# Spreading the last tokens' decays by a TensorE product, and a step's order with its 64-column products together

## The chip, the cores and the metric

The kernel runs on one core of a Trainium2 chip, in one launch. The metric is device time in microseconds (us), the median of three runs. The engines are named as in the profile: PE is TensorE, DVE VectorE, ACT ScalarE, POOL GpSimd and SP the engine that issues most DMAs; PEld is PE's loading of weights.

## What is computed

A gated linear attention over 4 sequences of 768 tokens with 8 heads of 40 columns, then a layer in which each token goes through one of 8 experts, then a gated layer. The change touches only the attention:

```python
for t in range(S):
    kt, vt, qt = (k[:, :, t], v[:, :, t], q[:, :, t])
    m_new = np.maximum(f_gate[:, :, t] + m, i_gate[:, :, t])
    f_stab = np.exp(f_gate[:, :, t] + m - m_new)
    i_stab = np.exp(i_gate[:, :, t] - m_new)
    m = m_new
    C = f_stab[:, :, None, None] * C + i_stab[:, :, None, None] * np.einsum('bhd,bhe->bhde', vt, kt)
    n = f_stab[:, :, None] * n + i_stab[:, :, None] * kt
    h_tilde = np.einsum('bhde,bhe->bhd', C, qt)
    nq = np.einsum('bhd,bhd->bh', n, qt)[:, :, None]
    denom = np.maximum(np.abs(nq), 1.0)
    y[:, :, t] = o * h_tilde / denom
```

## The kernel before

The attention is cut into 24 chunks of 128 tokens, 6 to a sequence. Within a chunk the recurrence becomes products: a matrix of decays between the chunk's tokens, computed on PE from two tables `at` and `rt` (`dec`, L636), goes through exp on ACT (`exp`, L640) and is multiplied on DVE (`pf`, L650) with the products of keys and queries (`sc`, L645). The result meets the values (`out`, L668). What earlier chunks left in the state C is added (`inter`, L677) after it was scaled on DVE (`gs`, L683), and the chunk's own share of the new state is the product `state` (L689). ACT scales the old state by the decay of the chunk's last token (`Cm`, L695, from the tile `gt`), DVE adds the new share (`C`, L703), ACT copies the sum into the layout that `inter` reads (`cb`, L710). Then come the denominators (`abs` L714, `den` L717), the output gate on POOL (`sod`, L722), the result x (L730), its rounding to f16 on ACT (`xh`, L734), the rest in two pieces on POOL and DVE (`xla` L737, `xl` L740), a transposition by five products on PE (`tr`, L746), its copy by ACT (`ev`, L750) and the router's logits (`log`, eight products of L123, and `lg`, L757).

`dec`, `sc`, `out` and their companions work on half of the heads at a time, so they stand twice in a step, as 0 and 1. The products `out`, `inter` and `state` have weights of 64 columns; they go in pairs, one for each half of PE's columns. All other products of a step have weights of 128 columns.

A step n runs all 18 kinds of work once, each for the chunk n minus a lag. The table `ORDER` gives the order and the lags by hand: `out0:1` is `out` for the first half of the heads of the chunk before. Every engine takes its part of a step in this order. `r:k` lets the routing of earlier tokens go on by k small operations, `scat` issues a scatter of finished rows on POOL.

The decays are prepared at the start for two halves of the tokens, x = 0 and 1 (`gates`). `store(x)` writes them to DRAM in two arrays, `L_d` (L516) and `a_d` (L517), from which `decay` loads the tables `at` (L415, L419) and `rt` (L421). `exps(x)` applies exp; its last lines write the decay of each chunk's last token to the DRAM array `G_d` (L529, on ACT's queue) and read it back on SP's queue, broadcast to 64 partitions, twice, into `gt` (L531). `to_end(x)` transposes what is needed by token, with products (L538) and two DVE copies (L540). Chunks 0 and 1 take their decays from SBUF; from chunk 2 on `dec` reads `at` and `rt`, from chunk 3 on their second half (x = 1). In the generator `rest()`, which the `r` entries advance, `store(1)` comes in step 1, and `exps(1)` with the loads of the second half right behind it at that step's end. SP issues in program order, one DMA behind the other.

PSUM tiles of `tr`, `log`, `state`, the routing and `to_end` share two slots (`psC`); `inter` and `out` write into one of two tiles `po`.

Of the kernel before, what the change touches and what calls it, by code (L numbers as in the profile page):

```python
# [9 lines left out]
F32 = mybir.dt.float32  # L10
# [4 lines left out]
ALU = mybir.AluOpType  # L15
# [4 lines left out]
B, H, S, D = 4, 8, 768, 40  # L20
R = B * H
T = 128
NC = S // T
NP = H // 2
# [5 lines left out]
E, F1, F2 = 8, 1024, 1536  # L30
# [7 lines left out]


ORDER = """  # L40
    r:1 tr:3 dec0:0 sc0:0 ev:3 r:2 exp0:0 out0:1 dec1:0 r:1 C:1 sc1:0 pf0:0 sod:2 r:1 x:2 kw:0 r:1 cb:1
    out1:1 exp1:0 r:1 log:3 scat:0 xh:2 r:1 inter:0 pf1:0 abs:1 lg:3 gs:0 state:0 xla:2 r:1 Cm:0 xl:2 den:1
"""
TMAX = (NT - MOST) // T + 1
PITCH = NT + MOST + T
# [14 lines left out]
def fused(ctx, tc, a, out, dbg=None):  # L60
    nc = tc.nc
    V, G, A, PE, SP_ = nc.vector, nc.gpsimd, nc.scalar, nc.tensor, nc.sync
# [3 lines left out]
    perm = ctx.enter_context(tc.tile_pool(name="perm", bufs=1))  # L66
    dram = ctx.enter_context(tc.tile_pool(name="dram", bufs=1, space=DRAM))
# [4 lines left out]
    small = ctx.enter_context(tc.tile_pool(name="small", bufs=2))  # L72
# [4 lines left out]

    c16 = perm.tile([128, 3, 128], F16, name="c16")
    tri, ones, ident16 = (c16[:, i, :] for i in range(3))
    c32 = perm.tile([128, 128 + (NC + 1) * E], F32, name="c32")  # L80
    ident = c32[:, 0:128]
    rev = c32[:, 128:128 + NC * E].rearrange("p (t e) -> p t e", e=E)
    ebase = c32[:, 128 + NC * E:]
    tok = perm.tile([128, NTILE + 1], U32, name="tok")
    ctab = perm.tile([1, E, 2 * TMAX + 4], F32, name="ctab")
    num_e, last_e, one_e, slots_r = (ctab[:, :, 2 * TMAX + i] for i in range(4))
# [16 lines left out]
    lg = perm.tile([128, NTILE, 2 * E], F32, name="lg")  # L103
# [267 lines left out]
    with ExitStack() as att:  # L371
# [4 lines left out]
        psC = att.enter_context(tc.tile_pool(name="psC", bufs=2, space=PSUM))  # L376

        tm = a1.tile([128, 2, 2, NC // 2, R], F32, name="tm")
        gt = a1.tile([128, 2, B, NP, NC // 2], F32, name="gt")
# [77 lines left out]
        fg, ig = fi[:, 0], fi[:, 1]  # L457
# [4 lines left out]
        c3 = lambda t: t.rearrange("p (c t) -> p c t", t=T)  # L462
# [1 line left out]

        a_d = dram.tile([2, NP, 2 * B, S], F16, name="a_d")
        L_d = dram.tile([2, 2 * B, NP * (LR + T)], F16, name="L_d")
        G_d = dram.tile([2, B, 2, NP * (NC // 2)], F32, name="G_d")
        half = lambda x: slice(x * S // 2, (x + 1) * S // 2)
        HC = NC // 2

# [54 lines left out]
        def exps(x):  # L525
            h = half(x)
            A.activation(ig[:, h], ig[:, h], AF.Exp)
            A.activation(fg[:, h], fg[:, h], AF.Exp)
            A.dma_start(out=G_d[x].rearrange("b j (p c) -> (b j p) c", c=HC), in_=c3(fg[:, h])[:, :, T - 1])  # L529
            for j in range(2):  # L530
                SP_.dma_start(out=gt[64 * j:64 * j + 64, x].rearrange("q b p c -> q b (p c)"),  # L531
                              in_=G_d[x:x + 1, :, j].to_broadcast([64, B, NP * HC]))

        def to_end(x):
            pg = psC.tile([128, 2, HC, R], F32, name="pg", tag="c")
            for k, t in enumerate((ig, fg)):
                for c in range(HC):
                    PE.transpose(pg[:, k, c, :], t[:, (x * HC + c) * T:(x * HC + c + 1) * T], ident[:R, :R])  # L538
            for j in range(2):
                V.tensor_copy(tm[:, x].rearrange("q k c (b p j) -> q (k c b) p j", j=2, p=NP)[:, :, :, j],  # L540
                              pg.rearrange("q k c (b j p) -> q (k c b) j p", j=2, p=NP)[:, :, j, :])

        blank = small.tile([1, 8], F32, name="blank", bufs=1)
        DIRECT = 2
# [2 lines left out]
        def begin():  # L547
# [31 lines left out]
            store(0)  # L579
            decay(0, 0, HC)  # L580
            exps(0)
            load_qk(chunks[2])
            load_v(chunks[2])
# [253 lines left out]
        def routing(k):  # L837
            for _ in range(k):
                if next(step.route, None) and not step.drain:
# [3 lines left out]
                     x=x, xh=xh, xla=xla, xl=xl, tr=tr, ev=ev, log=log, lg=lg_)  # L843
# [62 lines left out]
        def step(n):  # L906
# [15 lines left out]
            for name, lag in order:  # L922
# [6 lines left out]
                elif name in ("tr", "ev", "log", "lg") and n >= NTILE or name == "kw" and n == 0:  # L929
                    pass  # L930
                elif 0 <= n - lag < NTILE:
                    if n == NTILE - 1 and name == "xl":

                        mem = Within(hids[0], psS, psC, ("pw", "c"))
                        step.job = Head(mem, step.row, HEAD, lambda ins: tc.add_to_no_dep_group("first rows", ins.ins))
                    parts[name](chunks[n - lag])
                    if n == NTILE and name == "xl":

                        assert not pending or pending[-1][0] < EARLY
                        blank_rows(first_end(), SLOTS[0] - HEAD)  # L940
                    if n == 0 and name == "exp0":
                        step.route = rest()
                    if n == 0 and name == "pf0":
                        to_end(0)
                        kw(chunks[0])
                    if n == 0 and name == "exp1":
                        A.activation(gate(0), gate(0), AF.Sigmoid)
                        A.activation(blank, blank, AF.Exp)
                    if n == 2 and name == "pf0":
                        to_end(1)  # L950
                    if n < B - 1 and name == "state":
                        output_gates(n + 1, G)
                    if n >= (NTILE - 1 if name != "sod" else 20) and name in ("kw", "sod", "xla"):
                        out_of(1)
                    if n == NTILE and name == "x":
                        step.job.sums()
                    if n == NTILE and name == "out1":
                        step.posts, step.done = [step.job.up(f) for f in range(4)], 0
# [221 lines left out]
    with ExitStack() as m1:  # L1180
# [47 lines left out]
        with tc.manual_schedule(engines=manual):  # L1228
# [20 lines left out]
            for k, (r, s, n) in enumerate(jobs):  # L1249
# [13 lines left out]
                if k == E - 1:  # L1263

                    gs = [Group(0)]
# [74 lines left out]
def _constants():  # L1340
    p, t = np.arange(128)[:, None], np.arange(128)[None, :]
    c16 = np.stack([p < t, np.ones((128, 128)), np.eye(128)], axis=1).astype(np.float16)
    c32 = np.zeros((128, 128 + (NC + 1) * E), np.float32)
    c32[:, :128] = np.eye(128)
    c32[:, 128:128 + NC * E] = np.tile(E - np.arange(E), NC)
    c32[:, 128 + NC * E:] = PITCH * np.arange(E)
    k, u = np.arange(64)[:, None], np.arange(64)[None, :]
    cat = np.zeros((97, 2, T), np.float16)
    cat[8:32] = 1.0
    cat[32:96, 0, 0:64] = k == u  # L1350
    cat[32:96, 1, 64:128] = k == u
    cat[96, 0, 64:128] = 1.0
    crt = np.zeros((97, NP, T), np.float16)
    for h in range(8):
        crt[h, h % 4] = 1.0
    crt[32:96] = np.tile(np.where(k > u, -60000.0, 0.0), 2)[:, None, :]
    crt[96, :, 0:64] = -60000.0
    tok = (np.arange(128)[:, None] + 128 * np.arange(NTILE + 1)[None, :]).astype(np.uint32)

    ctab = np.zeros((1, E, 2 * TMAX + 4), np.float32)  # L1360
    ctab[..., :TMAX] = T * np.arange(TMAX)
    ctab[..., TMAX:2 * TMAX] = np.arange(TMAX)
    ctab[..., 2 * TMAX] = np.arange(E)
    ctab[..., 2 * TMAX + 1] = E - 1 - np.arange(E)
    ctab[..., 2 * TMAX + 2] = 1.0
    ctab[..., 2 * TMAX + 3] = SLOTS
    return {"c16": c16, "c32": c32, "cc": np.concatenate([np.concatenate([cat, crt], axis=1), np.zeros((31, 2 + NP, T), np.float16)]),
            "own_row": np.repeat(np.eye(H, dtype=np.float16)[:, :, None], T, axis=2), "tok": tok, "ctab": ctab}
# [18 lines left out]
def build(nc, arrays, dbg_shapes=None):  # L1387
    args = {n: nc.dram_tensor(f"in_{n}", x.shape, mybir.dt.from_np(x.dtype), kind="ExternalInput").ap() for n, x in arrays.items()}
    out = nc.dram_tensor("out_0", (NT, DM), F32, kind="ExternalOutput").ap()
    dbg = None  # L1390
    if dbg_shapes:
        dbg = {n: nc.dram_tensor(f"dbg_{n}", s, d, kind="ExternalOutput").ap() for n, (s, d) in dbg_shapes.items()}
    with tile.TileContext(nc) as tc:
        fused(tc, args, out, dbg)
# [11 lines left out]
```

## Time and profile before

| | |
|---|---|
| time, median of 3 runs (range) | 759.05 us (757.47 to 759.56) |
| time of the profiled execution | 757.82 us |
| its span, first to last instruction | 756.0 us |
| attention, 0 to 182.7 us: PE busy, its granted clock | 154.69 us, 0.88 |
| experts, 182.7 to 388 us | 200.16 us, 0.99 |
| gated layer, 388 to 756 us | 362.51 us, 1.00 |

A granted clock of 1.00 is PE at 2.4 GHz, 0.50 is 1.2 GHz. PE is busy for 95% of the span, so the stretches in which it is not, or not at full clock, are what a change can take away without removing work; they lie nearly all in the first stage. DVE is busy for 52%, ACT 44%, POOL 16%.

### The profile page before, as it was taken

How to read it: one execution, taken by the hardware profiler on the slowest of the kernel's cores; microseconds unless marked ns; L12 is line 12 of the kernel's file. 1: busy time of each engine (PE TensorE's matmuls, PEld its weight loads, DVE VectorE, ACT ScalarE, POOL GpSimd, SP SyncE). 2: the span in 40 equal slices, each digit the busy share in tenths (PEclk: the TensorE clock that was granted, in tenths of full speed). 3: DMA queues.
4: the chain of work that ended last, by engine and by line, in shares of the span. 5: the costliest groups of instructions: out<-in, count | busy, mean ns of one | idle time of the engine just before them, and what ended most of it. 6: DMA issues, size and time to landing. Idle time of an engine off the chain costs nothing. (4 is left out here: it accounts for less than half of the span.)

```text
span 756.0 us, 15468 instructions
## 1 busy us (share of the span) xinstructions
PE 717.4 (95%) x6075; PEld 504.1 (67%) x6075; DVE 389.7 (52%) x916; ACT 331.3 (44%) x763; POOL 121.5 (16%) x152
## 2 busy tenths in 40 slices
PE   8946999998899999999998999999999999999998
PEld 5736888887675667566765667666666666666665
DVE  5633465575578887898886970240312313133130
ACT  4428566664547665655454640231322313132231
POOL 4412346464421111122110000000000000000000
PEclk7579899999999999999999999999999999999999
DMA  6663244465289999797353402101001020000000
GB/s 183 177 121 96 89 146 155 150 191 185 89 222 306 285 269 274 225 264 221 111 147 80 105 1 62 45 1 53 1 19 36 1 53 1 18 10 10 18 1 26
DMA packets 67720, 84.00 MB, mean 111 GB/s; under 512 B 42565, under 2 KB 49942, under 8 KB 67646
## 3 DMA queue, kind: packets, MB, share of 16 engines
q1 hardware_dynamic: 63932, 70.59, 33.2%
q0 software_dynamic: 3056, 12.28, 5.2%
q8 instruction: 48, 0.79, 0.4%
q10 hardware_dynamic: 658, 0.14, 0.1%
q14 instruction: 26, 0.21, 0.1%
HBM read 57.51 MB, written 17.17 MB: 99 GB/s over the span
## 5 line engine op out<-in xcount | busy, mean ns | idle before, releaser
L123 PE MATMUL pa<-xT,wgv 128*128 128x384 f16 x1536 | 250.9, 326 | 2.1 <-DVE hh L1160 2.1
L123 PEld LDWEIGHTS <-wgv 128*128 128x128 f16 x1536 | 150.2, 98 | 101.3 <-issue 2.5
L1155 DVE SCALAR_TENSOR_TENSOR gt<-pa,sg 128x384 f32<-128x384 f32 x96 | 53.4, 556 | 223.3 <-PE pa L123 191.8
L1173 PE MATMUL pb<-wo,hh 128*128 128x320 f16 x864 | 118.5, 299 | 0.0
L1154 ACT ACTIVATE sg<-pa 128x384 f32<-128x384 f32 x96 | 47.0, 490 | 141.4 <-PE pa L123 141.3
L1173 PEld LDWEIGHTS <-hh 128*128 128x128 f16 x864 | 84.5, 98 | 33.2
L356 PE MATMUL pb<-w,hh 128*128 128x320 f16 (+4 forms) x624 | 87.2, 299 | 0.2
L123 PE MATMUL pa<-xT,w 128*128 128x384 f16 (+5 forms) x576 | 80.9, 301 | 2.4 <-DVE hh L346 2.4
L356 PEld LDWEIGHTS <-hh 128*128 128x128 f16 (+4 forms) x624 | 62.4, 101 | 23.6 <-DVE hh L346 1.9
L123 PEld LDWEIGHTS <-w 128*128 128x128 f16 x640 | 55.7, 98 | 33.3 <-issue 3.2
L650 DVE TENSOR_TENSOR pf<-ps,w 128x512 f32<-128x512 f32 x48 | 33.1, 690 | 56.3 <-PE ps L645 27.5
L110 DVE SCALAR_TENSOR_TENSOR w<-ws,w 128x512 f16<-128x512 f32 (+1 forms) x92 | 56.1, 639 | 6.4 <-ACT w L109 6.3
L109 ACT ACTIVATE w<-ws 128x512 f16<-128x512 f32 (+1 forms) x92 | 50.3, 592 | 16.4 <-DMA ws<-in_w 16.4
L645 PE MATMUL ps<-qk 128*128 128x128 f32 x384 | 57.5, 298 | 0.0
L1175 ACT ACTIVATE ob<-pb 128x320 f32<-128x320 f32 x24 | 10.5, 437 | 100.5 <-PE pb L1173 100.5
L645 PEld LDWEIGHTS ps<-qk 128*128 128x128 f32 x384 | 52.9, 213 | 1.6 <-issue 0.6
L1160 DVE TENSOR_TENSOR hh<-gt,hh 128x384 f16<-128x384 f32 x96 | 52.6, 548 | 0.7
L1159 ACT ACTIVATE hh<-gt 128x384 f16<-128x384 f32 x96 | 49.4, 515 | 6.0 <-DVE gt L1155 5.9
L367 POOL DMA_INDIRECT y_d<-yr,own x24 | 27.7, 1154 | 126.6 <-DVE u L1097 24.4
L640 ACT ACTIVATE w<-pw 128x512 f32<-128x512 f32 x48 | 28.5, 594 | 30.2 <-PE pw L636 23.5
L345 ACT ACTIVATE hh<-pa 128x384 f16<-128x384 f32 (+6 forms) x80 | 33.6, 432 | 13.9 <-PE pa L123 13.7
L346 DVE SCALAR_TENSOR_TENSOR hh<-pa,hh 128x384 f16<-128x384 f32 (+6 forms) x80 | 36.2, 477 | 5.2 <-ACT hh L345 5.0
(188 smaller groups left out, 701.1 us busy)
## 6 DMA issues: line engine op xcount, KB each, us to landing
ws<-in_w SPq DMA_DIRECT2D x24, 512.0 KB
vk<-in_vk SPq DMA_DIRECT2D x24, 324.0 KB
qk<-in_qk SPq DMA_DIRECT2D x48, 160.0 KB
ws<-in_w SPq DMA_DIRECT2D x15, 480.0 KB
ws<-in_wg SPq DMA_DIRECT2D x9, 512.0 KB
ws<-in_wv SPq DMA_DIRECT2D x9, 512.0 KB
hh<-in_o POOLq DMA_DIRECT2D x4, 960.0 KB, 9.6
ws<-in_wo SPq DMA_DIRECT2D x8, 480.0 KB
```

The lines of the kernel that those rows point to most:

```text
L109: A.activation(hi, src, AF.Copy, scale=scale)
L110: low = lambda: V.scalar_tensor_tensor(lo, src, scale, hi, ALU.mult, ALU.subtract)
L123: PE.matmul(ps, r if swap else l, l if swap else r, start=n == 0, stop=n == len(steps) - 1)
L345: A.activation(self.hh[:, 0, f], ph, AF.Relu)
L346: V.scalar_tensor_tensor(self.hh[:, 1, f], ph, 0.0, self.hh[:, 0, f], ALU.max, ALU.subtract)
L356: PE.matmul(py, self.hh[:, x, k, sl], w2[:, y, k, :], start=k == 0 and x + y == 0, stop=k == K1 - 1 and x == 1)
L645: PE.matmul(m.ps[g][:, p, :], m.k2[:, g, p], m.q2[:, p], start=True, stop=True)
L1154: A.activation(sg, pgv[0], AF.Sigmoid, scale=1.0 / (SY * SWG))
L1155: V.scalar_tensor_tensor(gt, pgv[1], SGT / (SY * SWV), sg, ALU.mult, ALU.mult)
L1159: A.activation(self.gh[:, 0, f, :], box[0], AF.Copy)
L1160: V.tensor_sub(self.gh[:, 1, f, :], box[0], self.gh[:, 0, f, :])
L1173: PE.matmul(po, self.gh[:, x, k, sl], wo[:, y, k * DM:(k + 1) * DM], start=k == 0 and x + y == 0, stop=k == K2 - 1 and x == 1)
```

## The change

`exps` loses its last lines: nothing is written to `G_d`, and `gt` isn't loaded. Instead `to_end(x)` lets DVE spread the decays of the chunks' last tokens over a block of columns, one for each sequence and pair of heads (the table `place_of`), multiplies that on PE with a table of ones (`side`) so that each partition gets the heads of its half, and copies the product to `gt` on DVE. The two tables come in the constant `c32`, whose load grows from 128x184 to 128x328 numbers. And `ORDER` is written anew: lags stay as they were but for `gs`, which goes from the step of its chunk to the start of the next.

```diff
 ORDER = """
-    r:1 tr:3 dec0:0 sc0:0 ev:3 r:2 exp0:0 out0:1 dec1:0 r:1 C:1 sc1:0 pf0:0 sod:2 r:1 x:2 kw:0 r:1 cb:1
-    out1:1 exp1:0 r:1 log:3 scat:0 xh:2 r:1 inter:0 pf1:0 abs:1 lg:3 gs:0 state:0 xla:2 r:1 Cm:0 xl:2 den:1
+    r:1 gs:1 C:1 tr:3 dec0:0 sc0:0 ev:3 r:2 exp0:0 sod:2 cb:1 dec1:0 sc1:0 r:1 pf0:0 kw:0 r:1 x:2 exp1:0
+    Cm:0 r:1 log:3 scat:0 xh:2 r:1 out0:1 pf1:0 r:1 out1:1 lg:3 xla:2 inter:0 state:0 r:1 xl:2 abs:1 den:1
 """
...
-            A.dma_start(out=G_d[x].rearrange("b j (p c) -> (b j p) c", c=HC), in_=c3(fg[:, h])[:, :, T - 1])
-            for j in range(2):
-                SP_.dma_start(out=gt[64 * j:64 * j + 64, x].rearrange("q b p c -> q b (p c)"),
-                              in_=G_d[x:x + 1, :, j].to_broadcast([64, B, NP * HC]))
...
+            own = small.tile([R, B * NP, HC], F32, name="own_g", bufs=1)
+            V.tensor_tensor(own, place_of.rearrange("r b p -> r (b p)").unsqueeze(2).to_broadcast([R, B * NP, HC]),
+                            c3(fg[:, half(x)])[:, :, T - 1].unsqueeze(1).to_broadcast([R, B * NP, HC]), ALU.mult)
+            pl = psC.tile([128, B * NP * HC], F32, name="pl", tag="c")
+            PE.matmul(pl, side, own.rearrange("r b c -> r (b c)"), start=True, stop=True)
+            V.tensor_copy(gt[:, x].rearrange("q b p c -> q (b p c)"), pl)
...
+    for r in range(R):
+        b, j, p = r // H, r % H // NP, r % NP
+        c32[r, 128 + (NC + 1) * E + 64 * j:][:64] = 1.0
+        c32[r, 2 * 128 + (NC + 1) * E + b * NP + p] = 1.0
```

What this makes of the engines' orders is shown at three places. Lines of the changed kernel are some 4 higher for the same work (L645 is L649 there). First PE in the middle of a step, from `sc1` of the step before to `sc0`; the tiles are `ps` for `sc`, `po` for `out` and `inter`, `pl` for `log`, `pu` for `state`, `pt` for `tr`, `pw` for `dec`. Before:

```order
L668 MATMUL po<-vk,pf_627 64x41 x8
L123 LDWEIGHTS xTu
...
L677 MATMUL po<-Cb_113,qk_110 64x82 x8
L689 MATMUL pu<-vk,kw_114 64x41 x8
L746 LDWEIGHTS xsb
...
L645 MATMUL ps<-qk_111 128x128 x4
L668 MATMUL po<-vk,pf_694 64x41 x8
L636 LDWEIGHTS at_105
...
```

And of the change:

```order
L649 MATMUL ps<-qk_110 128x128 x4
L125 LDWEIGHTS xTu
...
L672 MATMUL po<-vk,pf_587 64x41 x8
L672 MATMUL po<-vk,pf_618 64x41 x8
L681 MATMUL po<-Cb_113,qk_110 64x82 x8
L693 MATMUL pu<-vk,kw_114 64x41 x8
L750 LDWEIGHTS xsb
```

The products of 64 columns (those with 64 rows of output) stood in three places of a step and stand in one.

Second, the same step on DVE and then on ACT. DVE before, from `pf1` to the next step's `pf0`:

```order
L650 TENSOR_TENSOR pf_627<-ps,w_606 128x512
L683 TENSOR_TENSOR po<-po,tm 128x328
L740 TENSOR_TENSOR xsb<-x,xsb 128x64
L717 TENSOR_SCALAR den<-den 128x8
L718 RECIPROCAL den<-den 128x8
L703 TENSOR_TENSOR Cst<-Cm,pu 128x164
```

```order
L654 TENSOR_TENSOR pf_618<-ps,w_593 128x512
L744 TENSOR_TENSOR xsb<-x,xsb 128x64
L721 TENSOR_SCALAR den<-den 128x8
L722 RECIPROCAL den<-den 128x8
L687 TENSOR_TENSOR po<-po,tm 128x328
L707 TENSOR_TENSOR Cst<-Cm,pu 128x164
```

`xl` (the 128x64 operation) stood behind `gs` (128x328) and now stands ahead of it. ACT before:

```order
L640 ACTIVATE w_711<-pw 128x512
L734 ACTIVATE xsb<-x 128x320
L714 ACTIVATE den<-po 128x8
L757 ACTIVATE lg<-pl 128x16
L695 ACTIVATE Cm<-Cst,gt 128x41 x4
```

```order
L644 ACTIVATE w_698<-pw 128x512
L699 ACTIVATE Cm<-Cst,gt 128x41 x4
L738 ACTIVATE xsb<-x 128x320
L761 ACTIVATE lg<-pl 128x16
L718 ACTIVATE den<-po 128x8
```

`Cm` was ACT's last work in a step and now stands ahead of `xh` (the write of `xsb`).

Third, SP's queue where the second half of the decays is stored and loaded. Before:

```order
L433 DMA vk<-in_vk 128x648
L516 DMA L_d<-w_121 32x3x128
L517 DMA a_d<-w_121 8x4x384
...
L531 DMA gt<-G_d 64x4x12 x2
L419 DMA at_105<-a_d 8x2x384 x2
L421 DMA rt_107<-L_d 8x1x1536 x2
L429 DMA qk_110<-in_qk 40x1024
```

```order
L435 DMA vk<-in_vk 128x648
L517 DMA L_d<-w_121 32x3x128
L518 DMA a_d<-w_121 8x4x384
...
L421 DMA at_105<-a_d 8x2x384 x2
L423 DMA rt_107<-L_d 8x1x1536 x2
L431 DMA qk_110<-in_qk 40x1024
```

The two loads of `gt` are gone from between the stores and the loads of `at` and `rt`; the same happens in the first half.

## Rows read from the trace of the kernel before

**Rows 1.** The page's 40 equal slices: granted PE clock, in tenths.

```profile
PEclk7579899999999999999999999999999999999999
```

**Rows 2.** Timeline, PE, one step: start us, us, engine, line, work, [idle before].

```profile
58.34 0.70 PE L746 MATMUL pt<-c,xsb 128*128 128x128 f16 x5
...
59.10 1.05 PE L645 MATMUL ps<-qk 128*128 128x128 f32 x8
60.09 0.67 PE L668 MATMUL po<-vk,pf 128*64 128x41 f32 x16
60.69 0.39 PE L636 MATMUL pw<-rt,at 97*128 97x256 f16 x2
...
61.91 0.67 PE L668 MATMUL po<-vk,pf 128*64 128x41 f32 x16
...
63.96 0.70 PE L746 MATMUL pt<-c,xsb 128*128 128x128 f16 x5
```

**Rows 3.** Timeline, PE, moments of that step: the products that run then.

```profile
59.88 0.28 PE L645 MATMUL ps<-qk 128*128 128x128 f32 x1
...
60.52 0.24 PE L668 MATMUL po<-vk,pf 128*64 128x41 f32 x2
...
63.35 0.23 PE L677 MATMUL po<-Cb,qk 128*64 128x82 f32 x1
63.41 0.38 PE L689 MATMUL pu<-vk,kw 128*64 128x41 f32 x8
```

**Rows 4.** Timeline, PEld and DVE, at the same step's start.

```profile
58.43 0.21 DVE L740 TENSOR_TENSOR xsb<-x,xsb 128x64 f16<-128x64 f32 x1
...
58.70 0.17 PEld L746 LDWEIGHTS <-xsb 128*128 128x128 f16 x3 [0.24 <-DVE xsb L740]
```

**Rows 5.** Waits of PEld, 78 to 181 us: total us, times, longest us.

```profile
PEld L746 <- DVE xsb L740: 3.8, 11, 0.7
PEld L746 <- DVE rows_e L800: 2.6, 3, 0.9
```

**Rows 6.** Timeline, PE: first product of step 7, first of step 24.

```profile
83.94 0.23 PE L746 MATMUL pt<-c,xsb 128*128 128x128 f16 x1
...
180.24 0.26 PE L668 MATMUL po<-vk,pf 128*64 128x41 f32 x2 [0.61 <-DVE po L683]
```

**Rows 7.** Timeline, SP's queue: the second half of the decays.

```profile
34.71 0.66 SPq L517 DMA_DIRECT2D a_d<-w  x1
44.82 1.32 SPq L531 DMA_DIRECT2D gt<-G_d  x2
46.25 1.18 SPq L419 DMA_DIRECT2D at<-a_d  x2
```

**Rows 8.** Waits of SP's queue, 0 to 90 us: total us, times, longest us.

```profile
SPq L419 <- DMA a_d<-w: 7.5, 1, 7.5
...
SPq L531 <- DMA G_d<-w: 5.1, 1, 5.1
```

**Rows 9.** Timeline, ACT's queue and PE: the store of `G_d`, PE's long wait.

```profile
31.13 0.56 ACTq L529 DMA_DIRECT2D G_d<-w  x1
...
51.58 0.58 PE L636 MATMUL pw<-rt,at 97*128 97x256 f16 x2 [10.46 <-DMA rt<-L_d]
```

**Rows 10.** Timeline, PE, step 5: its wait for ACT.

```profile
72.60 0.38 PE L123 MATMUL pl<-wgl,xTu 128*128 128x16 f16 x8 [4.42 <-ACT xTu L750]
```

**Rows 11.** Timeline, ACT and POOL: the work between `tr` and the next `tr`.

```profile
59.08 0.70 ACT L750 ACTIVATE xTu<-pt 128x640 f16<-128x640 f16 x1 [0.74 <-PE pt L746]
...
62.35 0.67 POOL L737 TENSOR_TENSOR xsb<-x,xsb 128x256 f16<-128x256 f32 x1 [1.90 <-ACT xsb L734]
...
62.98 0.98 ACT L695 ACTIVATE Cm<-Cst,gt 128x41 f32<-128x41 f32 x4
...
71.87 0.68 ACT L750 ACTIVATE xTu<-pt 128x640 f16<-128x640 f16 x1
...
74.25 0.47 ACT L734 ACTIVATE xsb<-x 128x320 f16<-128x320 f32 x1
```

More of the change, by code (lines that the diff above doesn't have):

```diff
@@ L79, in fused @@
     tri, ones, ident16 = (c16[:, i, :] for i in range(3))
-    c32 = perm.tile([128, 128 + (NC + 1) * E], F32, name="c32")
+    c32 = perm.tile([128, 2 * 128 + (NC + 1) * E + B * NP], F32, name="c32")
     ident = c32[:, 0:128]
     rev = c32[:, 128:128 + NC * E].rearrange("p (t e) -> p t e", e=E)
-    ebase = c32[:, 128 + NC * E:]
+    ebase = c32[:, 128 + NC * E:128 + (NC + 1) * E]
+    side = c32[:R, 128 + (NC + 1) * E:2 * 128 + (NC + 1) * E]
+    place_of = c32[:R, 2 * 128 + (NC + 1) * E:].rearrange("r (b p) -> r b p", p=NP)
     tok = perm.tile([128, NTILE + 1], U32, name="tok")
@@ L466, in fused @@
         L_d = dram.tile([2, 2 * B, NP * (LR + T)], F16, name="L_d")
-        G_d = dram.tile([2, B, 2, NP * (NC // 2)], F32, name="G_d")
         half = lambda x: slice(x * S // 2, (x + 1) * S // 2)
@@ L1342, in _constants @@
     c16 = np.stack([p < t, np.ones((128, 128)), np.eye(128)], axis=1).astype(np.float16)
-    c32 = np.zeros((128, 128 + (NC + 1) * E), np.float32)
+    c32 = np.zeros((128, 2 * 128 + (NC + 1) * E + B * NP), np.float32)
     c32[:, :128] = np.eye(128)
     c32[:, 128:128 + NC * E] = np.tile(E - np.arange(E), NC)
-    c32[:, 128 + NC * E:] = PITCH * np.arange(E)
+    c32[:, 128 + NC * E:128 + (NC + 1) * E] = PITCH * np.arange(E)
+    for r in range(R):
+        b, j, p = r // H, r % H // NP, r % NP
+        c32[r, 128 + (NC + 1) * E + 64 * j:][:64] = 1.0
+        c32[r, 2 * 128 + (NC + 1) * E + b * NP + p] = 1.0
     k, u = np.arange(64)[:, None], np.arange(64)[None, :]
```

## The prediction

> **What bounds the kernel now.** I read the page first: PE is the engine with the most work, and the stretches where its clock stands at half lie at the start [rows 1]. So the question is PE's time in the attention, and I read its timeline there. Two things must be told apart: a step in which PE runs through, and the places where it waits.
>
> A step without a long wait took 63.96 - 58.34 = 5.62 us [rows 2], and the 17 steps from step 7 to step 24 took (180.24 - 0.61) - 83.94 = 95.7 us, 5.63 each [rows 6]. PE is nearly always at work in them, so other engines matter only where PE's own row names them. Inside the step the reader should look at the seams. The eight products of `sc` start 0.111 us apart: (59.88 - 59.10) / 7 [rows 2, 3]. The next start was due at 59.99, yet `out`, the first with 64 columns, starts at 60.09: 0.10 us lost. The eight pairs of `out` start 0.061 apart, (60.52 - 60.09) / 7; the next was due at 60.58, and `dec`, with 128 columns again, starts at 60.69: 0.11 lost [rows 2, 3]. Between `inter` and `state`, both of 64 columns, the start comes 0.06 us after the last pair's [rows 3]: nothing is lost. So what costs is the change of width. There are three stretches of 64 columns in a step, hence six changes.
>
> The second loss of a step: `tr` stops for 0.24 us until `xl` is done, which DVE starts late [rows 4]. In steps 7 to 23 this makes 3.8 us, and another 2.6 us are waits for a routing sum that frees `tr`'s PSUM slot [rows 5].
>
> The long waits: 10.46 us in step 3 for the table `rt` [rows 9], and 4.42 us in step 5, where ACT is busy with sigmoids [rows 10].
>
> **The steps' order.** One stretch of 64 columns instead of three: four changes fewer, 4 x (0.10 + 0.11) / 2 = 0.42 us; with the exposed start of a pair, which I can only see inside `out`, I take 0.43. In 17 steps that is 7.3 us. `xl` no longer stands behind `gs`: the 3.8 us go. The routing's sum now stands first in a step on DVE; but it needs an operation ahead of it that comes at the former step's end, so I let half of its 2.6 us go, 1.3 (bounds none and all).
>
> What is late next? PE's own work in a full step is then 5.62 - 0.24 - 0.43 = 4.95 us. Against it stands the chain through ACT, because `Cm` was moved ahead of `xh`: `ev` starts 59.08 - 58.34 - 0.24 = 0.50 after `tr` [rows 2, 4, 11]; from `ev` to `xh`, with both exps and `cb` between, it took 74.25 - 71.87 = 2.38 where ACT ran without a break; then `Cm` 0.98, `xh` 0.47, `xla` 0.67 [rows 11]. The sum is 5.00, and `xla` is wanted by the fourth product of the next `tr`, some 0.2 after its first, while hand-overs add about as much. So the chain asks for about 5.0 us a step and PE for 4.95: they are level. I charge 0.04 us for each of the 12 full steps, 0.5. In a sequence's first and last chunk `Cm` is absent, so the other 5 steps have room. `gs` at the next step's start has `tr`, both `dec`, both `sc` and `log` between it and `out`, the first that needs its result; the same work hides `C`.
>
> Steps 7 to 23: 7.3 + 3.8 + 1.3 - 0.5 = 11.9 us. Steps 3, 4 and 6 add three times 0.43, one of them at half clock and thus double, and one `xl` wait of 0.24: 1.9. In step 5 `out` now stands behind `log`, so PE has 1.2 us less to do before it waits for ACT, but does that work afterwards, where it waited again for the operands of `inter`; I take 0, bounds -1 and +1.2. Steps 0 to 2 end in PE's long wait, and what they gain is worth nothing.
>
> **The decays' spread.** Twice a DVE multiplication of 32x48, a product and a copy of 128x48 enter. The nearest rows are `xl`, 0.21 us for 128x64 [rows 4], and one product of `sc`, 0.111 [rows 3], so with a stop of PE between them about 0.5 us, at most 1, each time. Both lie in steps 0 and 2, ahead of the wait of 10.46 us, which covers them. If that wait were gone, they would cost up to 1 us. The larger load of constants is covered likewise.
>
> Removed are the store on ACT's queue and four loads on SP's. In the second half SP stands at the first load of `gt` until `G_d` has landed, 5.1 us of waiting that ends at 44.82; the loads take till 46.14, and `at` is issued at 46.25 [rows 7, 8]. PE starts at 51.58, 5.33 us after `at` [rows 7, 9]. Without `gt`, `at` waits for the stores of `a_d` and `L_d` alone. When have these landed? They were long done when asked, so the trace gives bounds only. The nearest row: in the first half the same wait took 7.5 us after the last store's issue [rows 8]; 34.71 + 0.66 + 7.5 = 42.9, and `rt` is there at 42.9 + 5.33 = 48.2: a gain of 3.4 us. The smallest gain: they landed with `G_d` at 44.82, and only the issue of `gt` goes: 46.25 - 44.82 = 1.4. The far end is stores that land at once: then all 10.46 us go. I take 3.4, since it is the same pair of transfers, and the first half had its own loads in the queues too.
>
> Here a rule speaks against the change. `G_d` is tiny, its store was issued at 31.13, and it landed only some 13 us later [rows 7, 9]. The Trainium skill ("DMA: Bandwidth & Descriptors", section "Queues, rings and completion order") says that a transfer's semaphore is counted up only once every earlier write of the same DMA engine has landed, whichever queue it came from. The trace agrees as far as these 13 us go. By that rule stores issued after `G_d` on the same engines can't be reported ahead of it, and the gain is 1.4, not 3.4.
>
> **The sum.** 11.9 + 1.9 + 3.4 = 17.2 us of the profiled execution's 757.82 (its span is 756.0): 740.6. The median of the runs is 1.23 higher: 741.8. Behind the attention nothing is changed, and I expect it to shift as a whole; how much of the clock's half level remains [rows 1] I leave as it is, since both waits stay longer than the one of 4.42 us that was followed by half clock.
>
> **Rivals.**
> (a) The stores land no earlier than `G_d` did: 1.4 instead of 3.4, 743.8. For it: the 13 us above. Against it: fewer small transfers are ahead in the queues.
> (b) The chain through ACT and POOL binds the step with 5.5 us, since each hand-over between engines costs 0.1 more than I see: 12 x 0.5 = 6 less, 747.8. For it: the levels are equal already. Against it: ACT ran `ev` to `xh` without a gap.
> (c) The change doesn't do what it says: the loss at a seam belongs to the first loads of `out`, not to the width, and comes along. Then 7.3 and 1.7 fall away: 750.8. Against it: the loss of 0.11 on leaving `out`.
> (d) Slower: the same chain, with `xla` also queued on POOL behind a scatter and `xh` on ACT behind a late `Cm`. The price is the chain's excess over 5.62 in 12 steps. The other 5 steps keep 0.5 each, steps 3, 4 and 6 their 1.9, and the wait gives 1.4 at least; together 5.8, so it decides from 5.62 + 5.8 / 12 = 6.1 us a step. At 6.3 it gives 2.4 us more than before: 761.4. Against it: 1.1 us above what the rows add up to.
>
> **How the numbers follow.** Forecast 0.56 (own range 736 to 746), (a) 0.16, (b) 0.12, (c) 0.05, (d) 0.05; 0.04 for a much earlier landing of the stores, which would give up to 7 us more, 734.8; 0.02 for a cause that I don't see and that cancels the gain. The prediction is 741.8. The range runs from 734 (stores at once) to 750 (case (b), with the bounds of step 5); (c) and (d) are left out. A measurement of this kernel can tell about 0.3% from no change, 2.3 us: faster by more has 0.56 + 0.16 + 0.12 + 0.05 + 0.04 = 0.93, slower 0.05, within it 0.02.
>
> **What would show it.** In the profile after, a full step of 4.9 to 5.1 us, with `sc0` followed by `dec1` after 0.11 us and one loss of 0.1 on entering and leaving the 64-column stretch; `tr` without waits for `xl`, perhaps with short ones for `xla`; PE's wait for `rt` ending near 48 with SP's wait before `at` now for `a_d` or `L_d`; step 5 about as long as it was. The prediction is wrong if the step stays above 5.3, if PE's waits move to `xla` or `lg` in most steps, or if the wait for `rt` ends outside 41 to 50.5.

## The result and the profile after

The changed kernel takes 735.92 us (median of 4 runs, 733.7 to 739.26) beside 759.3 us of the kernel before (4 runs): a ratio of 0.970, 95% interval [0.966, 0.974]. A second measurement gave 735.23 us and 0.968 [0.965, 0.971] (run after_again, below). The prediction was 741.8 us with a range of 734 to 750, so the sign and the range hold, and the gain is some 6 us larger than forecast. The profiled execution took 733.7 us, with a span of 731.6.

The page's slices of the granted clock, which answer to [rows 1], look much the same; this view is too coarse for what follows:

```profile
PEclk8698999999999999999999999999999999999999
```

One step of PE without a long wait, from the timeline (start us, us, engine, line, work, [idle before]); it answers to [rows 2, 3]:

```profile
44.44 0.45 PE L750 MATMUL pt<-c,xsb 128*128 128x128 f16 x5
44.73 0.39 PE L640 MATMUL pw<-rt,at 97*128 97x256 f16 x2
44.96 1.06 PE L649 MATMUL ps<-qk 128*128 128x128 f32 x8
45.85 0.39 PE L640 MATMUL pw<-rt,at 97*128 97x256 f16 x2
...
48.80 0.61 PE L693 MATMUL pu<-vk,kw 128*64 128x41 f32 x16
49.34 0.47 PE L750 MATMUL pt<-c,xsb 128*128 128x128 f16 x5
```

The step takes 49.34 - 44.44 = 4.90 us instead of 5.62. The last of the eight `sc` starts at 44.96 + 7 x 0.111 = 45.74, and `dec` follows 0.11 later: no loss where there were two, into `out` and out of it. The last pair of `state` starts at 48.80 + 7 x 0.061 = 49.23, and `tr` 0.11 later, where the next pair would have been due after 0.06; the loss on leaving the narrow stretch now stands once in a step. Of `tr`'s waits [rows 5] the view of PEld's waits from 65 to 149 us keeps one line, for the routing's sum; the one for `xl` is gone:

```profile
PEld L750 <- DVE rows_e L804: 1.0, 3, 0.3
```

SP's queue at the second half of the decays, then PE's rows with idle time from there to step 6, answering to [rows 7, 9, 10]:

```profile
32.63 0.66 SPq L518 DMA_DIRECT2D a_d<-w  x1
34.56 0.64 SPq L421 DMA_DIRECT2D at<-a_d  x2
```

```profile
34.93 0.39 PE L544 MATMUL pl<-own_g,c 32*128 32x48 f32 x2 [0.71 <-DVE own_g L541]
...
37.97 0.38 PE L640 MATMUL pw<-rt,at 97*128 97x256 f16 x2 [0.17 <-DMA rt<-L_d]
...
43.27 0.79 PE L681 MATMUL po<-Cb,qk 128*64 128x82 f32 x16 [1.66 <-DVE x L734]
...
57.46 0.38 PE L125 MATMUL pl<-wgl,xTu 128*128 128x16 f16 x8 [5.41 <-ACT xTu L754]
```

The long wait is gone. `at` is issued 34.56 - 33.29 = 1.3 us after the last store's issue ended, where it took 46.25 - 35.37 = 10.9 before; PE waits 0.17 us for `rt` where it waited 10.46. Two small waits are new: the product of the spread stops PE for 0.71 us (in step 0 as well as here in step 2), and `inter` in step 3 for 1.66 us, since DVE's `x` is now the last to come.

Where did the time go? The table cuts both profiles at the same work: `tr` at the start of steps 3, 4, 5, 6 and 7, and the start of step 24.

| stretch | predicted | first profile | after_again |
|---|---|---|---|
| up to step 3 | 0 | -3.08 | -0.94 |
| step 3 (17.91 us before) | -3.8 | -10.82 | -10.82 |
| step 4 (5.62) | -0.7 | -0.72 | -0.71 |
| step 5 (11.70) | 0 | -0.28 | -0.27 |
| step 6 (8.28) | -0.9 | -3.64 | -3.78 |
| steps 7 to 23 (95.69) | -11.9 | -12.05 | -12.04 |
| from step 24 on (576.37) | 0 | +6.18 | +6.46 |
| span | -17.2 | -24.4 | -22.1 |

Steps 4, 5 and 7 to 23 came as forecast. Step 3 is the decays' spread, with a part that is the clock. The three other differences are the clock, as the view by stretches shows (us, PE busy and instructions, PEld, DVE, ACT, POOL, granted clock of PE, DMA share, GB/s). First before: up to step 3, step 3, step 6, and from the first expert's products on:

```profile
0.00:40.43 40.43, 35.42 (x307) 27.17 (x307) 23.72 (x43) 18.68 (x37) 17.07 (x28) 0.70 0.67 174
40.43:58.34 17.91, 7.39 (x100) 6.47 (x98) 6.33 (x16) 4.42 (x14) 2.81 (x6) 0.71 0.55 117
75.66:83.94 8.28, 7.88 (x84) 6.85 (x82) 3.20 (x10) 2.51 (x6) 2.08 (x3) 0.57 0.14 42
182.72:756.00 573.28, 562.68 (x3793) 370.70 (x3793) 292.56 (x633) 226.16 (x492) 45.62 (x46) 1.00 0.35 99
```

And after:

```profile
0.00:37.35 37.35, 34.20 (x311) 25.60 (x311) 24.77 (x48) 18.80 (x38) 15.89 (x27) 0.77 0.60 189
37.35:44.44 7.09, 5.26 (x100) 4.92 (x97) 7.06 (x15) 4.08 (x12) 4.09 (x7) 1.00 0.87 279
60.77:65.41 4.64, 4.64 (x83) 4.47 (x82) 2.99 (x6) 2.51 (x6) 2.08 (x3) 0.93 0.50 146
152.91:731.60 578.69, 567.52 (x3793) 372.35 (x3793) 292.98 (x633) 226.54 (x493) 41.98 (x46) 0.99 0.35 99
```

Up to step 3 PE had 0.77 of its clock instead of 0.70, in step 6 0.93 instead of 0.57. In step 3 it had 1.00 instead of 0.71, and was busy for 5.26 us instead of 7.39 with the same 100 products. In e1 below, which keeps the old order, it is busy for 5.68 us there, also at 1.00; so 0.4 us of the 2.1 are the order and 1.7 the clock: the half clock that stood behind the long wait is gone with it. Behind the attention the same 3793 products took 5.4 us longer, of which PE was busy 4.8: more stretches at half clock.

### The profile page after: what moved, and what is told of

Its sections match the earlier page's. It is cut to its first block, busy times and chain, and to the rows that moved or that the text cites. A ratio compares the mean times of both kernels' runs of the same rounds, so it can differ in the third digit from the quotient of the medians.

```text
span 731.6 us, 15438 instructions
## 1 busy us (share of the span) xinstructions
PE 706.3 (97%) x6079; PEld 498.2 (68%) x6079; DVE 401.2 (55%) x920; ACT 328.3 (45%) x763; POOL 118.1 (16%) x152
## 5 line engine op out<-in xcount | busy, mean ns | idle before, releaser
L125 PE MATMUL pa<-xT,w 128*128 128x384 f16 (+5 forms) x576 | 82.6, 305 | 2.8 <-DVE hh L348 2.8
L649 PE MATMUL ps<-qk 128*128 128x128 f32 x384 | 53.8, 285 | 0.0
L649 PEld LDWEIGHTS ps<-qk 128*128 128x128 f32 x384 | 49.1, 200 | 1.4 <-issue 0.8
```

The source lines that it names most:

```text
L125: PE.matmul(ps, r if swap else l, l if swap else r, start=n == 0, stop=n == len(steps) - 1)
L649: PE.matmul(m.ps[g][:, p, :], m.k2[:, g, p], m.q2[:, p], start=True, stop=True)
```

## The experiments

Times stand as ratio to the kernel before, run on the same chip beside each; 0.01 is 7.6 us. In the code, `...` stands for lines left out.

### The two parts apart

e1 is the changed kernel with the old `ORDER`; e2 the kernel before with the new one.

```diff
 ORDER = """
-    r:1 gs:1 C:1 tr:3 dec0:0 sc0:0 ev:3 r:2 exp0:0 sod:2 cb:1 dec1:0 sc1:0 r:1 pf0:0 kw:0 r:1 x:2 exp1:0
-    Cm:0 r:1 log:3 scat:0 xh:2 r:1 out0:1 pf1:0 r:1 out1:1 lg:3 xla:2 inter:0 state:0 r:1 xl:2 abs:1 den:1
+    r:1 tr:3 dec0:0 sc0:0 ev:3 r:2 exp0:0 out0:1 dec1:0 r:1 C:1 sc1:0 pf0:0 sod:2 r:1 x:2 kw:0 r:1 cb:1
+    out1:1 exp1:0 r:1 log:3 scat:0 xh:2 r:1 inter:0 pf1:0 abs:1 lg:3 gs:0 state:0 xla:2 r:1 Cm:0 xl:2 den:1
 """
```

> The kernel before with the decays' spread by the product alone; the order of a step is the old one. Theory A (the two parts add up): the wait for rt in step 3, 10.46 us before, falls under 0.5 us, so that step 3's dec starts near 41.2 instead of 51.58; a full step stays at 5.62 us, and xl and the six changes of width cost what they did. Minus 10.3 us, less up to 2 us if PE's half clock takes up another stretch: 747 to 749 us against about 758. Rival B: the wait went because the order moved SP's and ACT's work, not because G_d went; then at is still issued after 44 us and the time is 756 to 759.

Measured: 752.61 us, ratio 0.987 [0.982, 0.992]. From the timeline of PE, the product of the spread, then `tr` of steps 3 and 4; and the stretch up to step 3:

```profile
38.80 0.39 PE L544 MATMUL pl<-own_g,c 32*128 32x48 f32 x2 [0.71 <-DVE own_g L541]
...
41.22 0.69 PE L750 MATMUL pt<-c,xsb 128*128 128x128 f16 x5
...
48.34 0.69 PE L750 MATMUL pt<-c,xsb 128*128 128x128 f16 x5
```

```profile
0.00:41.22 41.22, 36.55 (x311) 28.06 (x311) 24.35 (x47) 18.52 (x37) 16.41 (x28) 0.71 0.63 199
```

The clock stood as before up to step 3 (0.71 and 0.70), so the two profiles can be laid side by side: `tr` of step 3 starts 0.79 us later than before, at 41.22 instead of 40.43, which is the price of the added operations, and `tr` of step 4 starts at 48.34 instead of 58.34. The spread is worth 10.0 us by itself, without the order: 10.46 of waiting and 1.7 of half clock go, a stop of 1.38 us for `x` in step 3 and the 0.79 come. Rival B falls. A full step stays at 5.62 us. The median is 4 to 6 us over the 747 to 749 expected, which had been set against 758 us; the kernel before took 762.05 us beside it, and 9.4 us less than that is within the 9 to 11 forecast. In the profile, of the slowest run, the stretch from step 23 on took 590.4 us instead of 581.6, at a clock of 0.99 instead of 1.00 (more on this at e6).

> The kernel before with the new order of a step alone; the decays still go through G_d. Theory A: steps 7 to 23 take about 12 us less and steps 3, 4 and 6 1.3 to 1.9 less; the wait for rt still ends near 51.6 us, since SP stands at the load of gt until 44 to 45 us. 744 to 746 us. Rival B: the order also brings at forward, and the time is under 740. A full step is 4.9 us by both.

Measured: 750.56 us, ratio 0.987 [0.981, 0.992]. SP's queue, and PE's wait in step 3:

```profile
44.25 1.31 SPq L531 DMA_DIRECT2D gt<-G_d  x2
45.66 1.52 SPq L419 DMA_DIRECT2D at<-a_d  x2
```

```profile
51.26 0.58 PE L636 MATMUL pw<-rt,at 97*128 97x256 f16 x2 [11.52 <-DMA rt<-L_d]
```

With the order alone the wait ends where it ended before (51.26 and 51.58 us), and full steps take 4.90 us. So rival B falls here too: each part does its own work. The time missed the 744 to 746 us expected, and so did the gain, 11.5 us beside a kernel before of 762.05 instead of 12 to 14. In the profile steps 7 to 22 gained 10.8 us, 0.6 less than in the changed kernel, and from step 23 on it lost 6.2 us to before, with four pieces at half clock there where the trace of before has one (a stretch of double length counts as two, here and below). By the ratios the parts give 1.3% each and together 3.0 or 3.2%; with intervals of half a per cent they add up.

### The order's pieces

e3 moves only `gs` in the kernel before; e4 puts the two groups of `out` of the changed kernel back behind the two of `sc`.

```diff
-    r:1 tr:3 dec0:0 sc0:0 ev:3 r:2 exp0:0 out0:1 dec1:0 r:1 C:1 sc1:0 pf0:0 sod:2 r:1 x:2 kw:0 r:1 cb:1
-    out1:1 exp1:0 r:1 log:3 scat:0 xh:2 r:1 inter:0 pf1:0 abs:1 lg:3 gs:0 state:0 xla:2 r:1 Cm:0 xl:2 den:1
+    r:1 gs:1 tr:3 dec0:0 sc0:0 ev:3 r:2 exp0:0 out0:1 dec1:0 r:1 C:1 sc1:0 pf0:0 sod:2 r:1 x:2 kw:0 r:1 cb:1
+    out1:1 exp1:0 r:1 log:3 scat:0 xh:2 r:1 inter:0 pf1:0 abs:1 lg:3 state:0 xla:2 r:1 Cm:0 xl:2 den:1
```

> The kernel before with gs alone put at the start of the next step; out, inter and state stay apart, and the decays go through G_d. Theory A: xl no longer stands behind gs on DVE, tr's stop of 0.24 us goes in 16 steps: 3.8 us less, 753 to 755 us, full steps of 5.38 us. Rival B: DVE is late with xl for another reason, or gs at the start holds up C, cb and so inter: a full step stays at 5.6 us and the time at 757 to 759.

Measured: 755.17 us (10 runs, 749.86 to 758.56), ratio 0.991 [0.987, 0.994]. PE's timeline, `tr` of two steps that follow each other:

```profile
78.86 0.45 PE L746 MATMUL pt<-c,xsb 128*128 128x128 f16 x5
...
84.23 0.45 PE L746 MATMUL pt<-c,xsb 128*128 128x128 f16 x5
```

A full step takes 5.37 us, 0.25 less, and `tr` runs its five products in one piece (0.45 us, 0.70 in [rows 2]). The 16 steps from 7 to 22 take 84.48 us instead of 90.46: 6.0 us, more than the stops for `xl` alone, because the steps with routing also fell, from 6.70 to 5.53 us. Moving one 128x328 operation on DVE took away both waits of [rows 5]: the view of PEld's waits in these steps names neither.

```diff
-    r:1 gs:1 C:1 tr:3 dec0:0 sc0:0 ev:3 r:2 exp0:0 sod:2 cb:1 dec1:0 sc1:0 r:1 pf0:0 kw:0 r:1 x:2 exp1:0
-    Cm:0 r:1 log:3 scat:0 xh:2 r:1 out0:1 pf1:0 r:1 out1:1 lg:3 xla:2 inter:0 state:0 r:1 xl:2 abs:1 den:1
+    r:1 gs:1 C:1 tr:3 dec0:0 sc0:0 ev:3 r:2 exp0:0 out0:1 sod:2 cb:1 dec1:0 sc1:0 r:1 pf0:0 kw:0 r:1 x:2 out1:1 exp1:0
+    Cm:0 r:1 log:3 scat:0 xh:2 r:1 pf1:0 r:1 lg:3 xla:2 inter:0 state:0 r:1 xl:2 abs:1 den:1
```

> The changed kernel with the two groups of products of out put back behind the two of sc (out behind dec of the first half, and at the end of exp's second half), all else in the new order. Theory A (each change of width costs 0.10 to 0.11 us): four more changes a step, 0.43 us, so full steps of 5.33 us instead of 4.91, and in 20 steps 8 to 9 us more than the changed kernel's: 744 to 746 us. Rival B (the seam's loss belongs to out's first loads and not to the width, or other work hides it): 736 to 738 us.

Measured: 747.57 us, ratio 0.981 [0.976, 0.986]. PE's timeline of one step:

```profile
76.92 0.45 PE L750 MATMUL pt<-c,xsb 128*128 128x128 f16 x5
...
77.43 1.05 PE L649 MATMUL ps<-qk 128*128 128x128 f32 x8
78.42 0.67 PE L672 MATMUL po<-vk,pf 128*64 128x41 f32 x16
79.02 0.39 PE L640 MATMUL pw<-rt,at 97*128 97x256 f16 x2
...
82.29 0.45 PE L750 MATMUL pt<-c,xsb 128*128 128x128 f16 x5
```

The seams are back: `out` starts 0.21 us after the last `sc` (77.43 + 0.78) instead of 0.11, `dec` 0.17 after the last pair instead of 0.06. A full step takes 5.37 us, and steps 7 to 22 take 85.88 us instead of 79.08: 6.80 us in 16 steps, 0.425 a step, 0.106 for each of the four changes of width. Nothing else was changed, so rival (c) of the prediction, that the loss belongs to `out`'s first loads, falls. The Trainium skill ("TensorEngine Tiling (Array Packing)", section "Tiling Modes", key properties) says that TensorE drains when the tiling mode changes. The trace agrees, and adds the price.

### What made the wait of ten microseconds

Three candidates had left together: the store of 96 numbers of 4 bytes, the loads of `gt` with their small packets, and SP's standing at them. e5_store adds the old store, unread, to the changed kernel; e5_rows the same with rows of 12 bytes; e6 loads of the shape of `gt`'s from an input.

```diff
...
 A.activation(fg[:, h], fg[:, h], AF.Exp)
+A.dma_start(out=G_d[x].rearrange("b j (p c) -> (b j p) c", c=HC), in_=c3(fg[:, h])[:, :, T - 1])
```

> The changed kernel, and after each half's exp the old store of the last tokens' decays to G_d on ACT's queue (96 numbers of 4 bytes); nothing reads them, the product still fills gt. Theory A (the store itself holds up the landing of the stores issued around it): at is issued near 23 us in the first half instead of 18.13 and at 42 to 45 us in the second instead of 34.56, the wait for rt in step 3 is 7 to 10 us again, and the time is 742 to 747 us. Rival B (the loads of gt with their many packets of 48 bytes, or SP standing at them, made the wait): at stays at 18 and 34.6 us, and the time at 734 to 738.

Measured: 742.9 us, ratio 0.978 [0.973, 0.983]. SP's queue, and PE in step 3:

```profile
33.72 0.72 SPq L519 DMA_DIRECT2D a_d<-w  x1
41.27 0.65 SPq L421 DMA_DIRECT2D at<-a_d  x2
```

```profile
45.63 0.61 PE L642 MATMUL pw<-rt,at 97*128 97x256 f16 x2 [6.33 <-DMA at<-a_d]
```

The store alone brings back 6.33 us of waiting, a little less than the 7 to 10 expected. `at` is issued 6.8 us after the last store's issue ended, instead of 1.3 (1.26 or 1.27 in all seven traces of kernels that have the product and neither store nor loads); in the first half 7.0 us (22.01 - 14.96) instead of 2.1. The view of the DMA engines from 34 to 42 us, in 40 equal slices (busy share in tenths, GB/s), tells how:

```profile
DMA  9721131000000000000000000000009786073996
GB/s 259 204 82 59 53 108 35 12 0 0 0 0 0 6 1 0 0 0 0 0 0 0 0 0 0 0 0 0 0 0 269 77 115 115 0 233 154 461 422 269
```

From 35.4 to 40 us the engines are idle and next to nothing moves. So it isn't bandwidth that `at` waits for, but word that the stores have landed. The Trainium skill ("DMA: Bandwidth & Descriptors", section "Queues, rings and completion order") says that a transfer's count on its semaphore lands only after every earlier write of that DMA engine, from any queue. The trace agrees: stores on SP's queue are reported late because of a store on ACT's. The other 4.1 us of the old wait lie at the reading back of `G_d`: in the kernel before SP stood until 44.82, 9.45 us after its last store, and the loads of `gt` put `at` back by another 1.43 [rows 7].

```diff
...
+A.dma_start(out=G_d[x].rearrange("b j (p c) -> (b j p) c", c=HC), in_=fg[:, h][:, T - HC:T])
```

> As with the old store to G_d added to the changed kernel, but each of the 32 rows is written as one piece of 12 bytes (three tokens that stand side by side) instead of three of 4 bytes: as many bytes, a third of the writes. If the number of small writes sets the landing, the store costs a third of what the one with 96 writes costs: at near 37 to 38 us in the second half, a wait for rt of 3 us, 737 to 740 us. If one more store on ACT's queue costs it, whatever its shape, at is as late as with 96 writes. If stores don't matter at all, 734 to 738 us and at at 34.6.

Measured: 735.12 us, ratio 0.966 [0.961, 0.972]. SP's queue:

```profile
33.51 0.66 SPq L519 DMA_DIRECT2D a_d<-w  x1
36.24 0.64 SPq L421 DMA_DIRECT2D at<-a_d  x2
```

`at` follows after 2.1 us, and the kernel is as fast as without the store. As many bytes cost next to nothing as 32 writes of 12 bytes and 6.3 us as 96 of 4, and not a third of that, as the first theory expected. The 96 numbers are read from 96 separate places of SBUF and lie side by side in DRAM; whether their number, their size or the scattered reading decides was not tried.

```diff
...
+for j in range(2):
+    SP_.dma_start(out=g2[64 * j:64 * j + 64, x],
+                  in_=a["fi"][0:B, j, 0:NP * HC].unsqueeze(0).to_broadcast([64, B, NP * HC]))
```

> The changed kernel, and at the places of the old loads of gt on SP's queue four loads of the same shape (64 partitions, four sequences, 48 bytes each) from an input into a tile that nothing reads: the loads' packets without the store and without a wait for it. Theory A (the store made the wait): at is issued only the loads' own issue later, 1.3 us, near 36 us instead of 34.56; the wait for rt is 1 to 2 us and the time 735 to 739. Rival B (the many small packets hold up the stores' landing): at comes at 40 us or later, the wait is over 5 us and the time is over 741.

Measured: 733.2 us, ratio 0.965 [0.960, 0.970]. SP's queue, and PE in step 3:

```profile
32.80 1.37 SPq L532 DMA_DIRECT2D g<-in_fi  x2
34.33 0.75 SPq L422 DMA_DIRECT2D at<-a_d  x2
```

```profile
37.91 0.38 PE L644 MATMUL pw<-rt,at 97*128 97x256 f16 x2 [0.18 <-DMA rt<-L_d]
```

The loads cost nothing: their issue takes the place of the time in which SP waited anyway. Rival B falls.

The profile of e6 is of use for the clock as well. It runs like the changed kernel's up to step 23 (`tr` at 144.41 and 144.49 us), and then takes 583.7 us to its end instead of 587.1. PE stops for 2.14 us in the gated layer in both, as in the kernel before. The stretches behind that stop, of the changed kernel, its second profile (after_again), e6 and the kernel before:

```profile
385.33:388.70 3.37, 3.37 (x12) 1.63 (x13) 0.00 (x0) 0.90 (x2) 0.00 (x0) 0.56 1.17 264
```

```profile
389.32:392.70 3.38, 3.38 (x21) 2.07 (x22) 0.51 (x2) 0.90 (x2) 0.00 (x0) 1.00 1.18 253
383.71:387.10 3.39, 3.39 (x21) 2.07 (x22) 0.52 (x2) 0.90 (x2) 0.00 (x0) 1.00 1.24 230
```

```profile
411.52:414.90 3.38, 3.38 (x21) 2.07 (x22) 0.51 (x2) 0.90 (x2) 0.00 (x0) 1.00 1.06 267
```

The same stop before the same work is followed by 12 products, nearly all at half clock, once, and by 21 at full clock three times, one of them in the same kernel. The piece costs 1.7 us: from 385 to 390 us the granted clock is 0.66, and 0.34 x 5 is lost. In the traces the stretch from step 23 on has one such piece before (581.6 us), two in e6 and e9 (583.7 each), four in the changed kernel (587.1 and 587.4) and five in e1 (590.4). These pieces come and go with the same work.

e10 asks the converse: the new order with the way through DRAM kept, but the 32x3 numbers first copied side by side on ACT, so that the store has 32 writes.

```diff
...
-A.dma_start(out=G_d[x].rearrange("b j (p c) -> (b j p) c", c=HC), in_=c3(fg[:, h])[:, :, T - 1])
+ends = small.tile([R, HC], F32, name="ends", bufs=2)
+A.activation(ends, c3(fg[:, h])[:, :, T - 1], AF.Copy)
+A.dma_start(out=G_d[x].rearrange("b j (p c) -> (b j p) c", c=HC), in_=ends)
```

> The kernel before with the new order, and the decays still spread through G_d, without the product; but ACT first copies the 32x3 numbers side by side, so that the store to G_d is 32 writes of 12 bytes instead of 96 of 4. The loads of gt stay on SP's queue and wait for G_d. Theory A (the 96 writes of 4 bytes made most of the wait, not the way through DRAM): gt is loaded at 35 to 37 us instead of 44.25 with the new order alone, at follows 1.4 us later, the wait for rt falls from 11.52 to 1 to 4 us, and the time is 735 to 741 us, that of the changed kernel or a little over. Rival B (a store that is read back costs its landing in any case, since SP stands at it): gt is loaded after 41 us, the wait is 8 us or more and the time 747 to 751.

Measured: 744.46 us, ratio 0.979 [0.975, 0.982]. SP's queue, and PE in step 3:

```profile
36.23 1.32 SPq L533 DMA_DIRECT2D gt<-G_d  x2
37.65 0.81 SPq L419 DMA_DIRECT2D at<-a_d  x2
```

```profile
45.28 0.58 PE L638 MATMUL pw<-rt,at 97*128 97x256 f16 x2 [8.32 <-DMA rt<-L_d]
```

Both theories are half right. `gt` and `at` are issued 8 us earlier than in e2, so the writes of 4 bytes made most of that delay. But `rt` is there only 6 us earlier: it comes 7.6 us after `at`'s issue, where it took 3.4 in the changed kernel. POOL's load of 960 KB for the output gates is issued 1.2 us before `at` here (36.43), and 2.7 us after it in the changed kernel (37.27), so I take it for the cause; that was not tried by itself. The way through DRAM is still 7 to 8 us slower than the product.

### The added stop and the clock

> The changed kernel with DVE's multiplication by the table place_of put ahead of the transpositions and copies of to_end instead of behind them. Theory A (PE's two stops of 0.71 us for own_g come from DVE's order alone): both stops go, step 3 starts 0.7 to 1.4 us earlier, 734 to 735.5 us. Rival B (the product then waits for its PSUM slot, which DVE frees with the same copies): a stop of the same size with another releaser, 736 us.

e7 moves DVE's multiplication ahead of the transpositions in `to_end`. Measured: 737.66 us, ratio 0.969 [0.963, 0.975]: no difference that can be told. PE's timeline:

```profile
19.97 1.08 PE L693 MATMUL pu<-vk,kw 128*64 128x41 f32 x16 [0.92 <-POOL kw L662]
...
35.57 0.40 PE L544 MATMUL pl<-own_g,c 32*128 32x48 f32 x2
...
43.65 0.58 PE L640 MATMUL pw<-rt,at 97*128 97x256 f16 x2 [2.93 <-DMA rt<-L_d]
```

The two stops for `own_g` are gone, as theory A has it, but in step 0 a stop of 0.92 us for `kw` takes their place, and in step 3 the second half of `rt` came late, 7.35 us after `at`'s issue (36.30). POOL's load was issued 1.7 us behind `at` here, closer than in the changed kernel, which fits what e10 suggests and doesn't show it.

> The changed kernel with 26 products of constants (128x384, f16, result unused) ahead of log in step 5, in PE's wait of 5.41 us for the sigmoids on ACT. Theory A (the half clock from 54.6 to 61.5 us follows from PE's standing still there): the stretch goes, log to tr of step 6 takes 1.7 instead of 3.3 us, step 6 some 0.2 less, together 2 us less: 733 to 735 us. Rival B (the clock falls whatever PE does in that wait, as it does at the start): half clock stays in steps 5 and 6 and the time at 735 to 737.

> The changed kernel with three things together: the multiplication for own_g ahead of to_end's copies, the 26 products of constants in step 5, and 9 more ahead of the first expert's products in step 24, where PE stands for 2.1 us. Theory A (both stops of 0.71 us, and the half clock after both waits, go): 0.7, 2.0 and 1.7 us less, 730.5 to 733 us. Rival B (the clock's fall moves to the next wait, behind the attention): the granted clock falls elsewhere for as many stretches, 734 to 736 us.

> The changed kernel itself, on the same chip and beside the same runs of the kernel before. If the ratio of 0.970 belongs to the kernels and not to a chip's run, 0.966 to 0.974, 733 to 739 us; step 7 to step 24 takes 83.6 us again whatever the clock does at the start, and the first half-clock stretch starts anywhere between 11 and 13.7 us.

```diff
...
+def busy(n):
+    pz = psC.tile([128, 384], F32, name="pz", tag="c")
+    for _ in range(n):
+        PE.matmul(pz, c16[:, 0], c16.rearrange("p i t -> p (i t)"), start=True, stop=True)
...
+if n == 5 and name == "log":
+    busy(26)
...
+if n == NTILE and name == "out1":
+    busy(9)
```

e8 has the first call of `busy`, e9 both and e7's edit. On one chip: e8 735.23 us, 0.966 [0.963, 0.970]; e9 731.94 us, 0.965 [0.961, 0.969]; the changed kernel 735.23 us, 0.968 [0.965, 0.971]. The intervals overlap: e9 may be the fastest, but isn't shown to be. What the products do to the clock is shown. The stretch of e8 with steps 5 and 6, and the one before it:

```profile
46.92:57.15 10.23, 8.44 (x99) 7.73 (x98) 3.31 (x9) 4.70 (x13) 2.19 (x4) 0.55 0.29 87
57.15:72.25 15.10, 13.56 (x192) 11.05 (x189) 5.55 (x15) 12.56 (x20) 3.37 (x5) 1.00 0.28 89
```

In steps 5 and 6 the clock stays at full, 15.1 us for the two instead of 15.93 to 16.07. e9 keeps full clock there too, with 15.2 us, while the traces of all twelve kernels and repeats without these products have half clock behind that wait, of 4.0 to 5.4 us. So the half clock in these steps came from PE's standing still. But in e8's profile the clock had fallen earlier, behind the stop for `x` in step 3:

```profile
45.31 0.85 PE L687 MATMUL po<-Cb,qk 128*64 128x82 f32 x16 [1.55 <-DVE x L740]
```

With another 1.79 us of waiting for `qk`, step 4 then took 10.23 us instead of 4.91. The changed kernel has the same stop for `x`, with 1.66 us, and runs at full clock behind it (its step of 4.90 us above).

## Why the prediction was right, and where it was off

**Steps 7 to 23, right in size and in reason.** 11.9 us forecast, 12.05 and 12.04 measured. The width was put at 0.43 us a step; e4 gives 0.425. `xl` was put at 0.24, e3 gives 0.25. Two small terms were off in opposite directions: e3 gives 6.0 us in 16 steps for `xl` and the routing's sum, where 5.1 were charged in 17, and the rest of the new order, by subtraction, takes 1.4 of it back, where the chain through ACT and POOL was charged 0.5. A full step is 4.90 to 4.92 us (4.95 forecast), so rival (b) with 5.5 and rival (d) with 6.1 are far off.

**Steps 4 and 5, right.** 0.7 and 0 forecast, 0.72 and 0.28 measured.

**The wait for `rt`, wrong in size.** 3.4 us were taken out of bounds of 1.4 and 10.46; 10.3 went. The prediction had named a wait that ends outside 41 to 50.5 us as a sign of being wrong, and it ended at 37.97 (40.05 in the second profile): by its own test this term failed, though the time fell into the range. The failing step is the choice of the nearest row: the 7.5 us of the first half [rows 8] were read as what the stores need to land. They were what the stores need behind a store to `G_d`, which the first half had as well; without it the same wait is 2.1 us. In effect the row measured the thing that was to be removed.

**The rule, read the wrong way round.** Rival (a) held that stores issued after `G_d` can't be reported ahead of it, hence 1.4 us. e5_store bears out the order itself, with 6.8 us behind such a store and 1.3 without. But the change removes the store to `G_d`, so nothing is left to hold up the others: the order spoke for the far end of the bounds, which got a chance of 0.04. The 13 us between the store at [rows 9] and its landing were the clue; I took them for a delay that would stay when that store went.

**The added operations, right.** 0 while the wait covers them, up to 1 us if it is gone: it is gone, and e1 has 0.79.

**The clock, left as it was.** That failed in four places, three of them in favour. In step 3 the half clock went together with the wait that it followed, 1.7 us; the forecast had kept it, since it kept most of that wait. Step 6 gained 3.7 us instead of 0.9, because the half clock behind step 5's wait covers less of it. The start is scatter, -3.1 us in one profile of the changed kernel and -0.9 in the other; e3, where only `gs` is moved, has 37.33 us up to step 3, too, and e1 has 41.22. And from step 24 on 6.2 to 6.5 us were lost. The profile of before has the least half clock there of all kernels here, whose stretches from step 23 on lie between 581.6 us (before) and 590.4 (e1, with the old order); so I read its 576.37 us as a lucky draw rather than a base that the change made worse. The spans of 42 further runs of the kernel before, taken beside the experiments without a profile, go from 754.6 to 763.1 us with a median of 759.7, and seven are as short as the profiled 756.0; so the execution was a quick one, but where it was quick one profile can't prove.

Added up: 7.0 us more from step 3 (6.9 of the wait and 1.7 of the clock, less a new wait of 1.66 us for `x`), 2.8 more from step 6, 0.9 to 3.1 at the start, and 6.2 to 6.5 back behind the attention. So the time came out inside the range, near its low end, because errors of opposite sign met, and that is luck.

## What to carry to other kernels

When a wait is to be priced by a similar wait elsewhere, ask whether the thing to be removed stands in that row as well. A tiny store to DRAM of 4-byte elements that lie scattered in SBUF can delay the reported landing of all stores around it, on other queues too; gather the elements into rows first, or keep them on the chip. Products of the same weight width belong side by side in a step, and a late operation that one engine owes to another goes ahead of work that nobody waits for.

## What was not expected of the hardware

- 96 writes of 4 bytes held up the report of stores on another queue by 4.9 and 5.5 us, with the DMA engines idle for most of it; 32 writes of 12 bytes by 0.8 us at most.
- Whether half clock follows a short stop of PE isn't told by the stop's length here: 2.14 us were followed by it in one profile of the changed kernel and not in the other, 1.55 us in e8 and not 1.66 in the changed kernel. What else decides stays open. A piece like that in the gated layer costs 1.7 us, and these pieces are a part of the scatter between executions (733.7 to 739.26 us for the changed kernel).
- A change between products of 128 and 64 weight columns costs PE 0.106 us at full clock, the mean of four changes a step.
